# Layer 1 of a spectral/MLP block on one core: the d transform split by frequency modulo four, with new orders of work

## The chip, the cores and the metric

The kernel runs on one core of a Trainium2 chip. The metric is device time in microseconds (us): the median of six runs is 348.16 us (347.78 to 348.58). The core has TensorE (PE in the profile; PEld is its weight load), VectorE (DVE), ScalarE (ACT), GpSimd (POOL) and SyncE (SP, which only starts transfers).

## The reference

`x` is 2048 x 512 in bf16. Two kinds of layer alternate, twice each.

```python
x = A_x
x = x + _A_ref(_layernorm(x), A_w_r, A_w_i)
x = x + _B_ref(_layernorm(x), B_w1, B_w2, B_w3, B_w4)
x = x + _A_ref(_layernorm(x), A_w_r, A_w_i)
x = x + _B_ref(_layernorm(x), B_w1, B_w2, B_w3, B_w4)

def _A_ref(x, w_r, w_i):          # 2048 x 512 -> filter -> 2048 x 512
    X = rfft2(x.astype(float32))  # 2048 x 257 frequencies
    return irfft2(X * (w_r + 1j * w_i)).astype(bfloat16)

def _B_ref(x, w1, w2, w3, w4):
    h = gelu(layernorm(x) @ w1)                  # 512 -> 512
    hs = (four quarters of h, shifted by -1, +1, -2, +2 along 2048) @ w2
    x1 = x + hs
    return x1 + gelu(layernorm(x1) @ w3) @ w4    # 512 -> 1792 -> 512
```

"Layer 1" below is the first A and the first B; "layer 2" the second pair.

## The kernel before

The 2048 positions are written as 128 `p` times 16 `q`; a "row" q is a 128 x 512 tile, held in `K.x` for the whole kernel. The Fourier transforms are matrix products with tables. Layer A runs through six stages.

1. p transform (letter O in the orders). In layer 1 `first_front` takes the mean and variance of each row (s, i, f), the inverse deviation of a group of rows (S on ScalarE, J on VectorE), scales the table `T` by it (Q, on VectorE or ScalarE) and multiplies. `over_p` (L386 to L396) forms, for each of two blocks t of 128 columns, x[t]·T and x[t+2]·(T, -T) in one accumulation: the four matmuls of a row have 256 columns each and leave the sum and the difference of the two halves of the row. G (`take_V`) copies the result from PSUM into `V`, whose first index (four blocks of 128 d) is 2t + h, where h = 0 holds sums and h = 1 differences.
2. d transform (letter d, `over_d`, L504 to L512). Even frequencies need only the sums, odd ones only the differences, so for each of 16 frequency blocks b there are four matmuls of 256 columns (two h, two t) with the table `FA`. t copies the result to `TV`.
3. q transform (q, L535, table `TL` and its turned copy; x copies the result to `X`).
4. Filter (p, `weigh`, L554, VectorE only, weights `W`).
5. Inverse q (b, L565, table `TR`; m copies to `hT`), inverse d (D, L583, table `G`; Y copies) and inverse p (P, L595).
6. a adds the result to the row (L603); s, r, e, i, n form the next layer norm, T sends pairs of rows through a DMA transpose.

Blocks are handled in units: b = 0, 1, 14 and 15 alone ("singles"), the rest in pairs ("doubles"). Layer B then runs w1 (v, L635), w2 (u, L651), w3 (w, L686) and w4 (W, L706). Near its end the front of layer 2 is mixed in (the same letters O and G).

What runs when is written out by hand: `ORDER_0` (layer 1's front), `ORDER_A` (the rest of layer 1) and `ORDER_B` (layer 2) list operations as a letter, a number and, where there is a choice, the engine (V = VectorE, A = ScalarE). Each engine executes its own operations in that order and never overtakes. The number behind a point is the first PSUM bank. X is a number of filling matmuls on zeros (`fill`, 256 columns each); `WAKE` of them open the kernel and `FILL` puts some behind blocks of the first front.

Transfers: SyncE loads `x` (8 transfers), then the weights `W` (16), then, behind a gate that waits for the last part of W, `G`, `Tinv` and w1 to w4, then a dummy transpose. GpSimd's queue holds, in this order: the sums of rows 1 and 5, the loads of `FA`, `TL` (two halves) and half of `TR`, a doubling of the first quarter of `W` (a copy to the odd partitions), a gate that waits for the last scaled table, the turning of the first half of `TL` (L233, L234), the doubling of W's second quarter, the turning of the second half of `TL`, the last two doublings, and the rest of `TR`.

Rows 1 and 5 have their mean and square summed on ScalarE (`ON_ACT`, L349 and L285, finished by three small GpSimd operations); the other rows use VectorE's statistics instruction (L273, L301).

Of the kernel before, what the change touches and what calls it, by code (L numbers as in the profile page):

```python
# [28 lines left out]
def dft_tables():  # L29
# [27 lines left out]
    FA = np.stack([cos, -sin], axis=1).reshape(2, P, 2, P, 2)[..., ::-1].transpose(1, 0, 4, 2, 3)  # L57
    w = np.full(256, 2.0)
# [33 lines left out]
    out = {"T": np.stack([T, -T], axis=1), "FA": FA, "TL": TL, "TR": TR, "G": G, "G2": G2,  # L92
# [62 lines left out]
def load_all(K, A_x, A_w_r, A_w_i, B_w1, B_w2, B_w3, B_w4):  # L155
# [24 lines left out]
    def load_rest(after):  # L180
        q = nc.gpsimd
        load_TL = lambda k: q.dma_start(K.TL[:, 0, 8 * k:8 * k + 8], dram["TL"][:, 8 * k:8 * k + 8])
        load_TR = lambda k: q.dma_start(K.TR[:, 0:2 + k, 16 * k:16 * k + 16], dram["TR"][:, 0:2 + k, 16 * k:16 * k + 16])
        double = lambda k: q.dma_start(K.W[1::2, :, 8 * k:8 * k + 8], K.W[0::2, :, 8 * k:8 * k + 8])
        table("FA", q)
        load_TL(0)
        load_TL(1)
        load_TR(0)
        double(0)
        gate = K.const.tile([1, 2], BF16, name="gate")  # L190
        q.tensor_copy(gate[:], after[0:1, 0, 0:2])
        turn_TL(K, slice(0, 8))
        double(1)
        turn_TL(K, slice(8, 16))
        double(2)
        double(3)
        load_TR(1)

    K.load_rest = load_rest
    K.load_G2 = lambda: nc.sync.dma_start(K.G[:], dram["G2"])  # L200

    def load_mlp():
# [4 lines left out]
        for k, w, n, c in (("w1", B_w1, 4, D), ("w2", B_w2, 4, D), ("w3", B_w3, 4, FH), ("w4", B_w4, 14, D)):  # L207
            t = K.const.tile([P, n, c], BF16, name=k)
            nc.sync.dma_start(t[:], w.rearrange("(t p) n -> p t n", p=P))
            setattr(K, k, t)  # L210

# [185 lines left out]

def over_p_plain(K, qs):
# [34 lines left out]
def first_front(K):  # L433
# [30 lines left out]
    def front(k):  # L464
        ps[k] = over_p(K, FIRST[k], k == len(FIRST) - 1)
        if k in FILL:
            fill(K, FILL[k])

# [3 lines left out]
    def means(g):  # L472
        for i, q in enumerate(GROUPS[g]):
            if q in ON_ACT:
                L[g].from_means(i)

# [9 lines left out]
    spare = K.grp.tile([P, 4, 4, P], BF16, name="xT", bufs=4)  # L486
    K.nc.sync.dma_start_transpose(spare[:, 0, 0:1], K.zeros[:])


def layer(K, last):  # L490
# [13 lines left out]
    def over_d(u):  # L504
        bs = UNITS[u]
        ps["d", u] = o = banks(K, len(bs))
        for i, b in enumerate(bs):
            oi = o[:, i].rearrange("p (e h f) -> p h e f", e=2, h=2)
# [6 lines left out]
    def take_d(u, eng):  # L515
# [5 lines left out]
        else:  # L521
            copy(K, tv[u][:].rearrange("p n (e f h) -> p (n e) f h", e=2, h=2),
                 src.rearrange("p n (e h f) -> p (n e) f h", e=2, h=2), eng)
# [287 lines left out]
s0 s2 i0 s3 s1 i2 i3 f0 s4 S0 J0 i4 s5 Q1V Q0V Q3V Q2V s7 s6 i7 i6 s9 s11 O0 G0A f1 i9 S1 J1 s8 O1 G1A Q6A s10 Q7A i11  # L811
O3 i8 i10 Q5A s13 s12 Q4A O2 S2 J2 i13 Q10V G3A i12 Q9V s15 Q11A O5 S3 Q8A s14 i15 G2A O4 i14 S4 J3 Q12V G5A J4 Q15A
Q13V O6 Q14V G6A G4V O7 G7V O8 G8V G8A
"""
ORDER_A = """
X4.1 N0 d0.3 t0A d2.5 d1.7 t1A d4.0 t4A q0.2 x0A t2V q1.4 x1V p1 d10.6 d6.4 p0 t6V q2.1 t10A q4.6 x2A p2 x4A d12.3
b1.0 q6.1 p4 q10.6 t12A m1V b3.3 m3V x6A d8.4 d14.2 d15.0 x10A b5.6 t8A q8.4 p6 t14V t15A q12.0 b2.7 p10 m2V q14.2 m5A
x8A x12A q15.4 b0.6 m0A b10.7 m10A b4.1 m4A p8 b6.0 p12 m6V x14A p14 b11.7 x15A b9.1 p15 b13.6 m11A m9V m13A b7.3
b12.5 m12A b8.2 m8A b14.7 m14A m7V b15.5 m15A m15V D1.1 Y1V D0.5 D3.3 P2.7 a2 P3.2 a3 Y0A P0.1 a0 Y3A P7.4 P1.7 a1 s2
P6.2 s3 D2.0 s0 s1 a7 s7 a6 s6 D5.3 D4.6 r0 e0 Y2V P4.5 Y5A Y4A i0 n0V n1V P5.0 a4 s4 a5 s5 P11.2 D7.4 r1 P10.6 T0 Y7A  # L820
P8.3 e1 n3V n2V c1 T1 a11 a8 i1 D6.0 Y6A n5V P9.4 s11 P14.7 n4V n6V a9 n7V T2 P15.5 P12.3 a10 s8 a15 s9 a14 s10 P13.0
L0 v0.1 h0 a12 a13 v1.5 h1 T3 r2 c2 v3.4 n11V s12 c0 n10V T5 n8V n9V h3 s15 v2.3 h2 u0.5 L8 u3.0 u2.7 f0 L2 s14 f3
u1.5 f1 s13 r3 n12V n14V n15V f2 T4 v5.2 n13V h5 v4.1 u4.5 f4 E1 h4 u7.6 u6.1 f7 E3 u5.4 T7 k1 k0 f6 f5 k3 k2 E5 R0 c3
T6 v7.5 h7 u15.7 E0 v6.0 h6 E6 E4 u8.4 k7 o0V k5 o1V f15 E2 k6 o2V u10.3 o3V f10 k10 u12.7 u11.0 f8 u14.1 f14 U0 U1
u9.2 f9 k9 k8 w2.4 g2 f12 L9 E9 k4 R1 f11 k11 R2 w5.6 E11 g5 w4.2 g4 w1.0 u13.4 E8 o8V g1 o9V w3.5 g3 f13 E10 o10V
w0.1 g0 E7 o4A o7V w6.3 g6 W2.2 z0 o5V o6V A2 W3.7 A3 W1.6 A1 B1 W0.2 U3 U4 U2 E14 A0 w8.6 L13 B3 j3 g8 k14 o11V w12.1
g12 U5 w13.6 g13 w7.3 g7 w9.6 g9 k15 w10.3 g10 w18.0 w15.3 E12 g18 g15 w14.6 g14 w16.0 L11 w11.3 g11 g16 B2 W6.2 E13
W4.0 A6 w20.5 k13 L5 A4 B4 L12 W7.0 g20 w17.4 k12 R3 g17 o13A W5.1 A5 w19.5 g19 W9.2 o12V U6 j1 A7 B7 L15 j7 E15 j2 L7
o15V B6 W8.1 j6 B0 B5 j5 L3 W10.7 j0 S0 A10 B10 o14A U7 A9 j10 w25.4 g25 B9 Q2 j4 j9 A8 B8 L1 S1 Q1 Q4 w24.6 g24 W11.0
w21.2 g21 Q6 w22.6 j8 A11 L4 Q0 Q7 B11 j11 g22 L10 O0.3 w26.1 L14 g26 S2 Q11 G0A Q3 w23.6 w27.0 Q9 G0V g23 O1.2 G1A  # L830
Q10 G1V g27 W12.5 A12 O3.0 B12 W15.6 j12 Q5 G3A G3V A15 O2.2 G2A B15 Q8 j15 G2V S15 J15 Q15 W13.5 A13 B13 S12 W24.4
A24 j13 S13 J12 Q12 B24 J13 W14.5 Q13 A14 B14 O4.0 G4A O15.2 j14 S14 O5.6 G15V G15A O6.4 J14 Q14 O14.2 G4V G5A X3.7
G14V L6 G6A X4.1 G14A
"""
ORDER_B = """
d1.1 d4.3 t1V d15.7 t15V d8.0 t8V t4A q1.2 x1A p1 q4.6 x4A p4 d12.4 q15.2 t12A d10.6 x15A p15 t10A q8.0 q12.4 x12A
b1.2 m1A d14.6 d2.3 t14A x8V p12 t2A d0.0 t0A b5.2 m5A p8 q10.5 x10V p10 q2.3 x2A d6.0 t6A b9.2 p2 b4.3 m9A q0.4 x0A
p0 q14.6 m4A x14A q6.0 x6A b13.2 b12.4 m12A b10.3 b0.7 m0A p14 b3.5 m3A b2.0 m13A m10V p6 b14.3 b11.4 m2V b8.6 m11A
m8A b7.5 b6.4 m14V m6A m7V b15.1 m15A m15V D3.4 Y3A D2.6 D1.1 Y2A P6.3 a6 Y1A s6 D0.4 P4.6 Y0A P5.7 P7.3 a4 s4 P3.1 a5
s5 a7 s7 a3 r1 P2.0 a2 P0.7 a0 s3 P1.3 a1 s2 e1 i1 n4V D5.4 D7.1 D4.6 Y5A P11.3 P10.0 n5V D6.4 n7V n6V s0 s1 r0 Y7A e0  # L840
Y4V P8.6 P9.2 T2 P14.1 a10 i0 c1 n2V n3V Y6A s10 a11 n1V P15.0 n0A s11 a9 a8 s9 s8 c0 r2 T3 P13.7 a13 P12.5 a12 T1
v3.3 h3 v2.6 h2 s12 n10V T0 v1.2 n8V n9V T4 v0.4 s13 n11V h1 u3.7 a14 T5 h0 a15 u1.6 f1 u0.0 s15 u2.4 f2 s14 r3 n14V
n15V T7 n12V v5.2 h5 v4.1 h4 u4.5 n13V E1 k1 u6.4 f3 E3 f0 E0 u7.3 k2 u5.7 k3 k0 c2 f7 T6 v6.2 h6 v7.1 h7 E2 f5 u13.6
R0 u12.0 E7 o2V u14.7 o3V o1V f6 o0V c3 f12 U0 f13 u15.2 f15 k15 f4 f14 E14 E15 E6 k13 k12 u9.0 f9 u10.1 k14 U1 w2.4
g2 w4.6 k4 f10 R3 k10 E13 w0.1 g0 w6.3 E12 o12A g4 w1.1 g1 g6 w3.5 g3 w5.1 g5 u11.5 E4 k5 f11 W2.3 E11 o13V o14A k7 U6
o15A k11 W1.4 A1 k6 R1 u8.2 A2 f8 k9 k8 R2 o6V U7 w25.6 g25 w22.3 o4V E10 o10A g22 E5 o5V w21.0 W3.2 A3 g21 w24.5 g24
# [35 lines left out]
```

## Time and profile before

One execution was profiled. It took 347.91 us, of which the traced span is 346.1 us; the granted TensorE clock is 1.00.

| stretch (us) | what runs |
|---|---|
| 0 to 18.4 | loads, layer 1's front: statistics, p transform |
| 18.4 to 38.1 | layer 1's d, q, filter and inverse q |
| 38.1 to 52.8 | layer 1's inverse d and p, layer norm, transposes |
| 52.8 to 179 | layer 1's B, at its end layer 2's statistics and part of its p transform |
| 179 to 183.2 | the rest of layer 2's p transform |
| 183.2 to 202.8 | layer 2's d, q, filter and inverse q |
| 202.8 to 218.2 | layer 2's inverse d and p |
| 218.2 to 342.7 | layer 2's B |
| 342.7 to 346.1 | last addition and store |

In a timeline row the columns are start, length, engine, line, operation, output and inputs, count, and in brackets the idle time before it with what ended it. The length of a matmul row contains the drain of the last one, so the pitch is read from start to start.

### The profile page before, as it was taken

The numbers are of one execution on the slowest core, as the hardware profiler recorded it, in microseconds if no ns is written. First come the engines' busy times: TensorE is split into PE (matmuls) and PEld (weight loads), VectorE is DVE, ScalarE is ACT, GpSimd is POOL, SyncE is SP. The second block draws the span as 40 slices with busy tenths as digits, with TensorE's granted clock in tenths as the row PEclk, the third lists the DMA queues.
The fourth block names the chain that finished last, engine by engine and source line by source line (L and its number), as shares of the span: only waits on it lengthen the run. The fifth ranks groups of instructions, "written<-read, shape, count | busy, mean of one in ns | idle before, by whom it ended". The sixth has DMA issues, their size and how long they took to land.

```text
span 346.1 us, 5563 instructions
## 1 busy us (share of the span) xinstructions
PE 336.7 (97%) x2116; PEld 189.6 (55%) x2134; DVE 187.7 (54%) x452; ACT 192.0 (55%) x342; POOL 64.5 (19%) x158
## 2 busy tenths in 40 slices
PE   8899999999999999999999999999999999999996
PEld 6778884444444444444577888444444444444453
DVE  5979798785435012877698959666614202002012
ACT  5979799666505633124357989954784521350320
POOL 2470047442200001022000003544304000000000
PEclk9999999999999999999999999999999999999999
DMA  7998965430221000310000002542103114100101
GB/s 256 282 336 273 370 112 110 78 63 2 53 40 30 0 2 0 57 36 1 0 2 2 0 2 54 95 86 50 24 2 61 30 45 105 19 29 17 45 23 53
DMA packets 45337, 24.64 MB, mean 71 GB/s; under 512 B 34944, under 2 KB 42240, under 8 KB 45312
## 3 DMA queue, kind: packets, MB, share of 16 engines
q1 hardware_dynamic: 43904, 20.00, 23.4%
q0 software_dynamic: 1168, 4.20, 3.4%
q8 instruction: 16, 0.26, 0.3%
q10 hardware_dynamic: 240, 0.10, 0.2%
q14 instruction: 9, 0.07, 0.1%
HBM read 11.67 MB, written 2.10 MB: 40 GB/s over the span
## 4 chain that ended last, share of the span: by engine, by line
PE 78%; DMA 9%; DVE 7%; ACT 2%; SPq 1%; issue 1%; ACTq 0%; DVEq 0%; POOLq 0%
PE ps L686 28%; PE ps L706 27%; PE ps L635 8%; PE ps L651 8%; DMA W<-in_A_w_i_dram 4%; DVE x_state L603 3%; PE ps L511 2%; DMA xT<-xn 2%; PE ps L583 2%; DVE PB L554 1%; DMA W<-in_A_w_r_dram 1%; PE ps L535 1%; DMA W<-W 1%; ACT hT L152 1%; DVE xn L369 1%
## 5 line engine op out<-in xcount | busy, mean ns | idle before, releaser
L693 ACT ACTIVATE gT<-ps 128x1024 bf16<-128x1024 f32 x56 | 56.3, 1021 | 93.9 <-PE ps L686 93.7
L686 PE MATMUL ps<-xT,w 128*128 128x512 bf16 x448 | 99.3, 379 | 0.1
L706 PE MATMUL ps<-w,gT 128*128 128x512 bf16 (+1 forms) x464 | 97.8, 366 | 0.6
L712 DVE TENSOR_TENSOR x_state<-ps,x_state 128x512 bf16<-128x512 f32 (+1 forms) x34 | 22.1, 657 | 108.5 <-PE ps L706 106.8
L706 PEld LDWEIGHTS <-gT 128*128 128x128 bf16 x476 | 46.4, 98 | 49.9
L686 PEld LDWEIGHTS <-w 128*128 128x128 bf16 x448 | 43.8, 98 | 52.6 <-DMA xT<-xn 0.2
L659 DVE SCALAR_TENSOR_TENSOR xn<-xn,ln_c,ps 128x512 bf16<-128x512 bf16 x32 | 23.2, 743 | 21.5 <-PE ps L651 13.1
L635 PE MATMUL ps<-xT,w 128*128 128x512 bf16 x128 | 28.8, 379 | 1.0 <-DMA xT<-xn 1.0
L651 PE MATMUL ps<-w,hT 128*128 128x512 bf16 x122 | 28.6, 379 | 0.3
L285 ACT ACTIVATE junk<-xn 128x512 bf16<-128x512 bf16 x32 | 19.7, 620 | 10.0 <-DVE xn L659 10.0
L642 ACT ACTIVATE hT<-ps 128x512 bf16<-128x512 f32 x32 | 18.1, 600 | 11.8 <-PE ps L635 11.8
L603 DVE SCALAR_TENSOR_TENSOR x_state<-ps,x_state 128x512 bf16<-128x512 f32 x32 | 20.5, 686 | 5.1 <-PE ps L595 5.1
L273 DVE BATCH_NORM_STATS2 ln_st<-x_state 128x6 f32<-128x512 bf16 (+1 forms) x31 | 20.1, 665 | 3.4 <-DMA x_state<-in_A_x_dram 3.0
L635 PEld LDWEIGHTS <-w 128*128 128x128 bf16 x128 | 12.4, 98 | 16.2 <-issue 1.8
L651 PEld LDWEIGHTS <-hT 128*128 128x128 bf16 x128 | 12.5, 98 | 15.1
L291 POOL TENSOR_SCALAR ln_mv<-ln_s 128x4 f32<-128x4 f32 x16 | 4.9, 304 | 84.5 <-DVE x_state L603 72.4
L554 DVE TENSOR_TENSOR PB<-X,W 128x2048 bf16<-128x2048 bf16 (+1 forms) x20 | 19.6, 1008 | 0.7 <-ACT X L152 0.5
L285 ACT ACTIVATE xn<-x_state 128x512 bf16<-128x512 bf16 x32 | 19.8, 622 | 0.2 <-DVE x_state L603 0.2
L293 POOL TENSOR_TENSOR ln_mv<-ln_s,ln_t 128x4 f32<-128x4 f32 x16 | 3.7, 233 | 75.7 <-ACT junk L285 70.3
L583 PE MATMUL ps<-G,hT 128*128 128x256 bf16 x128 | 15.4, 272 | 0.9 <-DVE hT L150 0.8
L565 PE MATMUL ps<-TR,PB 128*128 128x128 bf16 x256 | 16.1, 219 | 0.1
L565 PEld LDWEIGHTS <-PB 128*128 128x128 bf16 x256 | 14.8, 98 | 1.5 <-issue 1.2
(87 smaller groups left out, 387.6 us busy)
## 6 DMA issues: line engine op xcount, KB each, us to landing
w<-in_B_w_dram SPq DMA_DIRECT2D x2, 1792.0 KB, 12.5
W<-W POOLq DMA_DIRECT2D x4, 514.0 KB, 4.6
x_state<-in_A_x_dram SPq DMA_DIRECT2D x8, 256.0 KB, 5.1
out_dram<-x_state SPq DMA_DIRECT2D x15, 128.0 KB, 1.8
w<-in_B_w_dram SPq DMA_DIRECT2D x2, 512.0 KB, 5.5
W<-in_A_w_r_dram SPq DMA_DIRECT2D x7, 128.5 KB, 7.1
W<-in_A_w_i_dram SPq DMA_DIRECT2D x7, 128.5 KB, 6.6
TR<-tab_TR POOLq DMA_DIRECT2D x1, 768.0 KB, 6.1
```

The lines of the kernel that those rows point to most:

```text
L285: K.nc.scalar.activation(out, src, ACT.Square, bias=0.0, scale=D ** -0.5, accum_out=self.s[:, i, 1:2])
L554: nc.vector.tensor_tensor(t, X.pop(u)[:, 0:2 * n].unsqueeze(1).to_broadcast([P, 2, 2 * n, 256]), K.W[:, :, 2 * u:2 * u + 2 * n, 1:257], op ...
L565: nc.tensor.matmul(oh, lhsT=pab[u][:, k, 2 * (b - u) + h, F * P:(F + 1) * P], rhs=K.TR[:, k:k + 2, 2 * b + h], start=(k == 0), stop=(k == 1))
L583: nc.tensor.matmul(o[:, i, e * 256:(e + 1) * 256], lhsT=M[:, F, e, 2 * m + i, :], rhs=K.G[:, F, e, :], start=(F == 0 and e == 0), stop=(F ...
L603: nc.vector.scalar_tensor_tensor(K.x[:, q, :], ps.pop(("P", q)), 1.0, K.x[:, q, :], op0=ALU.mult, op1=ALU.add, accum_out=ln[g].s[:, i, 0:1])
L635: nc.tensor.matmul(o[:, i], lhsT=K.w1[:, t, j * P:(j + 1) * P], rhs=xT[g][:, :, t, :], start=(t == 0), stop=(t == 3))
L651: nc.tensor.matmul(o, lhsT=K.hT[:, j, st:st + P], rhs=K.w2[:, j, :], start=(j == 0), stop=(j == 3))
L659: nc.vector.scalar_tensor_tensor(xn[:, q, :], xn[:, q, :], ln[q // 4].c[:, q % 4:q % 4 + 1], ps.pop(("u", n)), op0=ALU.mult, op1=ALU.add, ...
L686: nc.tensor.matmul(o[:, i], lhsT=K.w3[:, c, t * P:(t + 1) * P], rhs=xT3[g][:, :, c, :], start=(c == 0), stop=(c == 3))
L693: nc.scalar.activation(gT[g][:, 2 * j:2 * j + 2, :], ps.pop(("w", k)), ACT.Gelu_apprx_tanh, bias=0.0, scale=1.0)
L706: nc.tensor.matmul(o, lhsT=gT[g][:, t, i * P:(i + 1) * P], rhs=K.w4[:, t, d], start=(t == 0), stop=(t == 13))
L712: nc.vector.tensor_tensor(x, ps.pop(("W", n)), x, op=ALU.add)
```

## The change

Layer 1 only, arithmetic: the p transform adds the four quarters of a row in all the combinations that the d transform needs. `V` then holds x0 - x2, x0 + x1 + x2 + x3, x0 - x1 + x2 - x3 and x1 - x3. Frequencies 0 modulo 4 need one block of 128 d, frequencies 2 modulo 4 one block, odd frequencies two blocks. A row of the p transform has eight matmuls (four of 256 and four of 128 columns); a block b of the d transform has two of 128 and two of 256 columns.

```diff
+def over_p_quarters(K, qs, split=False):
+    ps = banks(K, 2 if split else len(qs))
+    for i, q in enumerate(qs):
+        T = K.Tq.pop(q)
+        plus, both, swap = T[:, 0], T[:], T[:, ::-1]
+        twice = lambda k: T[:, k:k + 1].to_broadcast([P, 2, P])
+        for h in range(2):
+            o = (ps[:, h, 0:256] if split else ps[:, i, h * 256:(h + 1) * 256]).rearrange("d (k p) -> d k p", k=2)
+            terms = ((0, o, twice(0)), (1, o[:, 1], plus), (3, o[:, 1], plus), (2, o, swap)) if h == 0 else \
+                    ((1, o, swap), (0, o[:, 0], plus), (2, o[:, 0], plus), (3, o, twice(1)))
+            for n, (c, dst, rhs) in enumerate(terms):
+                K.nc.tensor.matmul(dst, lhsT=K.x[:, q, c * P:(c + 1) * P], rhs=rhs, start=(n == 0), stop=(n == 3))
+    return ps
...
-        ps[k] = over_p(K, FIRST[k], k == len(FIRST) - 1)
+        ps[k] = over_p_quarters(K, FIRST[k], k == len(FIRST) - 1)
...
+            if not last:
+                oi = o[:, i].rearrange("p (e r f) -> p e r f", e=2, r=4)
+                part = lambda k: V[:, k, 2 * b:2 * b + 2].rearrange("d b q c -> d (b q c)")
+                nc.tensor.matmul(oi[:, :, 3], lhsT=part(1), rhs=K.FL[:, 0:P].rearrange("p (e f) -> p e f", e=2),
+                                 start=True, stop=True)
+                nc.tensor.matmul(oi[:, :, 1], lhsT=part(2), rhs=K.FL[:, P:2 * P].rearrange("p (e f) -> p e f", e=2),
+                                 start=True, stop=True)
+                for k in range(2):
+                    rhs = K.FL[:, (k + 1) * 256:(k + 2) * 256].rearrange("p (e r f) -> p e r f", e=2, r=2)
+                    nc.tensor.matmul(oi[:, :, 0:3:2], lhsT=part(3 * k), rhs=rhs, start=(k == 0), stop=(k == 1))
+                continue
```

The copies t of layer 1 read PSUM with four interleaved classes instead of two; their size stays. The new table `FL` (128 x 768, 192 KB) is loaded into a spare transpose buffer where `FA` (256 KB) was loaded, right behind the sums of row 5 on GpSimd's queue; `FA`, which only layer 2 uses now, comes on SyncE's queue behind w4. The turned second half of `TL` is loaded as a table of its own (`TL2`, 256 KB) instead of being formed by two GpSimd operations. Row 9's sums go to ScalarE, with three small operations on GpSimd ahead of the first doubling.

```diff
+    def load_tables():
+        spare = K.grp.tile([P, 4, 4, P], BF16, name="xT", bufs=4)
+        K.FL = spare[:, 0:2].rearrange("p a b c -> p (a b c)")[:, 0:768]
+        q.dma_start(K.FL, dram["FL"])
         load_TL(0)
         load_TL(1)
         load_TR(0)
...
         turn_TL(K, slice(0, 8))
         double(1)
-        turn_TL(K, slice(8, 16))
+        q.dma_start(K.TL[:, 1, 8:16], dram["TL2"])
         double(2)
         double(3)
...
-WAKE = 35
-FILL = {0: 3, 1: 3, 2: 2, 3: 2, 4: 2}
+WAKE = 30
+FILL = {}
-ON_ACT = [1, 5]
+ON_ACT = [1, 5, 9]
+TABLES = 1
```

All three orders are written anew. `ORDER_0` whole, and `ORDER_A` as far as the first D (the first lines of each):

```diff
 ORDER_0 = """
-s0 s2 i0 s3 s1 i2 i3 f0 s4 S0 J0 i4 s5 Q1V Q0V Q3V Q2V s7 s6 i7 i6 s9 s11 O0 G0A f1 i9 S1 J1 s8 O1 G1A Q6A s10 Q7A i11
-O3 i8 i10 Q5A s13 s12 Q4A O2 S2 J2 i13 Q10V G3A i12 Q9V s15 Q11A O5 S3 Q8A s14 i15 G2A O4 i14 S4 J3 Q12V G5A J4 Q15A
-Q13V O6 Q14V G6A G4V O7 G7V O8 G8V G8A
+s0 s3 s2 i3 s1 f0 i0 i2 S0 s5 f1 J0 Q0V Q1V Q2A Q3A s4 i4 s6 s7 i6 i7 O0 G0A S1 s10 J1 s12 Q6A s9 Q7V s13 i12 i13 Q4V
+s8 S3 O1 G1A Q5V O3 J3 O2 i10 G3A Q12V s11 i8 i11 Q13V O6 f2 S2 J2 G2A Q10V Q11V Q8V O5 G6A Q9A O4 s15 s14 i15 i14 S4
+J4 Q14V O7 G5A Q15V G4A O8 G8A G7V G8V
 """
 ORDER_A = """
-X4.1 N0 d0.3 t0A d2.5 d1.7 t1A d4.0 t4A q0.2 x0A t2V q1.4 x1V p1 d10.6 d6.4 p0 t6V q2.1 t10A q4.6 x2A p2 x4A d12.3
-b1.0 q6.1 p4 q10.6 t12A m1V b3.3 m3V x6A d8.4 d14.2 d15.0 x10A b5.6 t8A q8.4 p6 t14V t15A q12.0 b2.7 p10 m2V q14.2 m5A
-x8A x12A q15.4 b0.6 m0A b10.7 m10A b4.1 m4A p8 b6.0 p12 m6V x14A p14 b11.7 x15A b9.1 p15 b13.6 m11A m9V m13A b7.3
-b12.5 m12A b8.2 m8A b14.7 m14A m7V b15.5 m15A m15V D1.1 Y1V D0.5 D3.3 P2.7 a2
...
+d0.3 t0V d1.6 d2.0 t1A q0.2 x0V p0 t2A q1.4 x1A p1 d4.6 N0 t4A d10.1 t10A q2.4 x2V p2 q4.6 d6.0 x4A t6A d12.3 t12A
+d14.5 q10.6 q6.0 d8.2 p4 x10A b4.4 x6V b3.7 d15.6 t8A q8.2 m4A t15A p10 p6 q12.0 b1.4 m3A b0.6 b2.7 x8A x12A b6.2 m2A
+t14V b5.3 m1V p8 q15.0 m0A q14.4 b10.7 x15A b9.6 p12 m6A m10V p15 b8.0 m5A x14A b7.2 m7A b11.3 p14 b12.7 m8V b13.5 m9V
+b14.1 m11A m12A b15.2 m13A m14A X4.0 m15A m15V D1.5 Y1A D0.0 Y0A D3.3 Y3A P2.5 a2
...
```

`ORDER_B` has the same operations as before, in another order and with some copies t, x and m given to the other engine: ScalarE has 9 double copies, 16 copies of 512 columns and one half in layer 2's stretch from the first d to the first D, where it had 9, 17 and one half.

## Prediction

> **What bounds the kernel now.** I read the page's first part, then busy time by stage, then the timelines of TensorE, VectorE and ScalarE up to 40 us, last the chain of waits. Busy time by stage (stretch, its length, busy time and instructions of TensorE, weight load, VectorE, ScalarE, GpSimd; clock, DMA share, GB/s):
>
> ```profile
> 7.50:16.90 9.40, 8.14 (x70) 6.72 (x70) 9.29 (x33) 8.71 (x18) 4.28 (x10) 1.00 0.93 291
> 16.90:29.00 12.10, 11.82 (x130) 9.45 (x129) 10.27 (x14) 9.85 (x14) 6.94 (x8) 1.00 0.89 316
> 29.00:38.00 9.00, 8.64 (x141) 7.62 (x138) 8.95 (x12) 8.84 (x16) 0.00 (x0) 1.00 0.95 317
> 52.90:80.00 27.10, 27.00 (x124) 12.22 (x127) 21.01 (x60) 18.60 (x45) 13.84 (x33) 1.00 0.40 76
> ```
>
> From 52.9 us on TensorE alone is full, and the change leaves its matmuls there alone. Up to 38 us three engines are nearly full together: what one gives up counts only if the others follow. The matmuls in the timeline of TensorE:
>
> ```profile
> 7.56 0.27 PE L392 MATMUL ps<-Tq,x_state 128*128 128x256 bf16 x1 [0.47 <-DVE Tq L379]
> 11.30 0.27 PE L392 MATMUL ps<-Tq,x_state 128*128 128x256 bf16 x1 [1.18 <-ACT Tq L381]
> 17.50 0.27 PE L394 MATMUL ps<-Tq,x_state 128*128 128x256 bf16 x1
> 18.42 2.78 PE L511 MATMUL ps<-FA,V 128*128 128x256 bf16 x24
> 38.09 2.78 PE L583 MATMUL ps<-G,hT 128*128 128x256 bf16 x24 [0.46 <-DVE hT L150]
> ```
>
> So the front runs to 18.42, and d to the first D is 19.67 us. Pitches of matmuls come from pieces of the chain of waits, which follow without a gap (layer 2):
>
> ```profile
> 192.33 0.45 PE ps L565 x8
> 192.78 0.98 PE ps L535 x16
> 206.04 0.87 PE ps L583 x8
> ```
>
> 128 columns 0.056 us, 256 columns 0.109 us, the half-height q matmuls 0.061 us, weight loads hidden. TensorE's work in the 19.67 us is 64 x 0.109 (d) + 64 x 0.061 (q) + 128 x 0.056 (b) = 18.0 us, so 1.7 us of waits.
>
> ScalarE and VectorE (timelines):
>
> ```profile
> 7.03 0.87 DVE L379 TENSOR_SCALAR Tq<-T,ln_r 128x256 bf16<-128x256 bf16 x4
> 9.23 1.25 DVE L273 BATCH_NORM_STATS2 ln_st<-x_state 128x6 f32<-128x512 bf16 x2
> 19.12 0.60 ACT L152 ACTIVATE TV<-ps 128x512 bf16<-128x512 f32 x1 [0.91 <-PE ps L511]
> 24.19 1.94 ACT L152 ACTIVATE X<-ps 128x1024 bf16<-128x1024 f32 x2 [0.35 <-PE ps L535]
> 35.12 3.06 ACT L152 ACTIVATE hT<-ps 128x512 bf16<-128x512 f32 x6
> ```
>
> Start to start: statistics 0.59, scaled table 0.20 on VectorE and 0.42 on ScalarE, a double copy on ScalarE 0.91, a single one or an m 0.48. ScalarE's copies between 19.12 and 37.95 (letters t, x, m with an A): 10 doubles x 0.91 + 15 singles x 0.48 + a half of 0.35 = 16.65 us in 18.83 us, 2.2 us of waits.
>
> **The front.** Removed: twelve fills (1.3 us). Added: four 128-column matmuls per row; a row is now 4 x 0.109 + 4 x 0.056 = 0.66 us, where it was 0.44: 16 rows 10.6 us instead of 7.0. TensorE has idled or filled for about 3 us in its 10.2 us here, which would just hide the 3.6 us if the rows came evenly. They do not. I lay out `ORDER_0` by the pitches:
>
> - Row 0's table is the first to be scaled and J0 no longer stands behind s4: row 0 starts at about 7.28 (now 7.56), rows 0 and 1 end at 8.60, rows 2 and 3 (tables scaled on ScalarE behind row 5's sums, 8.0 to 8.85) at 9.94.
> - ScalarE copies G0A until 9.75, S1 to 10.05, J1 on VectorE 10.2, Q6A 10.75: row 6 starts at 10.8 (now 11.30).
> - From there twelve rows stand end to end: 12 x 0.66 = 7.9 us, and 0.2 for row 5, whose scaling stands behind s8: 18.9. Now the last row ends at 17.6. The statistics and scalings of VectorE end at 17.4 by the same pitches (14 changes to 13 statistics, 9 to 12 scalings) and are no longer last; row 9's two sums on ScalarE (1.3 us, by rows 1 and 5) lie in 10.75 to 12.05, where only G1A stands behind them, with 0.4 us left before row 12 needs its bank.
> - Last copies as now (17.72 to 18.42): d starts at 19.6, **1.2 us later**. Bounds: +0.6 if row 6 starts half a microsecond sooner, +1.8 if each of the three bank waits costs 0.2.
>
> No row has a matmul that adds 128 columns into half of an open accumulation. b's 128-column row (0.056) is the nearest; the 256-column pitch is the upper bound, +0.053 x 64 = 3.4 us. I take the nearest.
>
> The Trainium skill speaks against this step: "TensorE: Matmul & The Clock Gate", section "Back-to-back issue gap", gives about 81 ns per matmul of N=128 in a stream of weight load and matmul pairs. The trace's b stream is such pairs, at 0.056. By the page the front would be an estimated 1.6 us longer still; the measurement decides.
>
> **d to the first D, layer 1.** d loses 16 x (4 x 0.109 - 2 x 0.109 - 2 x 0.056) = 1.7 us, so TensorE's work is 16.3 us. But ScalarE now has 10 doubles, 16 singles and the half, 17.1 us, starting at 0.91 (d0, d1, 0.25 to the copy). Floor: 0.91 + 17.1 + 0.14 (last m to D) = 18.2. Laid out bank by bank ScalarE waits about 0.7 more: I take **18.9, 0.8 us less** than 19.67. Bounds: 18.2 and, with all of today's 2.2 us of waits, 20.4. Interleaving four classes on read is the same number of elements; between zero (the two-class copy has the same 0.91 as layer 2's plain one) and 0.23 each, the gap between VectorE's and ScalarE's double copy, for eight doubles: 1.8. I take zero.
>
> **Transfers and GpSimd.** Two turning operations go (1.66 + 0.78 us), a transfer comes (0.6 us of issue). GpSimd's queue: the three operations for row 9 (0.6 us) delay the first doubling to about 13; its user p0 runs at 22. What follows is the gate (16.3), the first turn (to 18.9, needed by q0 at 21), the second doubling, then `TL2` at 19.5; like `TL` (5.8 us to landing) it lands at 25.3. Its first user, q10, is at 19.6 + 6.6 = 26.2: hidden by 0.9 us, and a stall of 1.2 us if it takes the 7.9 us that half of `TR` took on this queue. The third doubling goes out 1.7 us sooner, or waits for W as now. `FL` is 64 KB smaller than `FA`. On SyncE, `FA` costs an issue of 0.5 us and, with `TL2`, 0.45 MB, at 350 GB/s 1.3 us of queue ahead of the dummy transpose; weights drain now at 45, the first transpose starts at 47.3, so it is covered by 2 us; uncovered, it delays w1 (52.8) one for one.
>
> **The rest.** From the first D to w1 the order of VectorE, which leads to the transposes, is the same but for Y1, which goes to ScalarE off the path: 0, bounds 0.4 either way. B is TensorE end to end with the same matmuls: 0. Layer 2's d to D has no new work; ScalarE's first copy comes at 2.0 instead of 1.57, with 16.2 instead of 16.7 us of copies: -0.1, bounds -0.5 to +0.5. Tail: the last store still follows the last addition (A20 before y20): 0.
>
> **Sum** against the profiled 347.91: +1.2 - 0.8 - 0.1 = +0.3, 348.2. The profiled run lies 0.25 under the median of 348.16; on the median 348.4. This kernel's runs tell about 0.2% (0.7 us) from no change, and +0.3 is inside.
>
> **Rivals.**
> 1. Faster. The columns taken from d pay in full and the front hides the added ones: front +0.6, stage at its floor (-1.5), layer 2's rewritten order -0.4: -1.3, 346.9. For: the 3 us of idling and fills in the front; TensorE's share in 18 to 38. Against: twelve rows end to end.
> 2. Slower. ScalarE is the bound of the stage. It has 0.5 us more copies and keeps today's waits: the stage is 20.1, +0.5, and the front's +1.2 is not returned: +1.6, 349.8. For: 16.65 of 18.83 us busy already. It decides once ScalarE waits over 1.3 us between first copy and D (stage 19.5, total +0.9).
> 3. Slower. `TL2` is late for q10: on top of the forecast up to 1.2 us, 349.6, once it needs more than 6.7 us to land.
> 4. The clock: fills are gone and TensorE idles about 0.7 us before 7.3 and 0.9 before 10.8. If the clock falls, some 3 us at half speed, +1.5: 349.9. Against: 1.18 us idle before 11.30 now, clock 1.00.
>
> **Numbers.** Forecast 0.38 (its own range 347.6 to 349.0), rival 1 0.32, rival 2 0.21, rivals 3 and 4 0.09 together. Range 346.5 to 350.2: the sums of rivals 1 and 4 and 0.3 beyond; costlier copies or matmuls lie outside. Faster 0.32, same 0.38, slower 0.30.
>
> **What would show it.** Right: d starts at 19.2 to 20.0 with rows end to end from about 10.8; the first D 18.6 to 19.2 later; q10 waits for no transfer; first w1 at 53.2 and the same distance from there to the end as now. Wrong: d before 19.0, a pitch of L424's matmuls over 0.66 per row, the stage under 18.2 or over 19.7, a clock below 1.00 before 20 us, or more than 0.5 us gained or lost behind w1.

## The result, and the profile after

The changed kernel took 348.87 us (median of 21 runs, 348.22 to 350.48); the kernel before, in 42 runs beside it, 348.28 us (347.71 to 350.13). The ratio is 1.0019 with a 95% interval of 1.001 to 1.0027: slower by some 0.6 us, at the 0.2% that this kernel's measurement can tell from no change. The forecast was 348.4, with a range of 346.5 to 350.2.

The execution that was profiled took 349.64 us, 0.77 above its own median, so its rows can't be set against those of before without care. Two things in it are chance, and shown below: its input came late, and its transposes were held. First the busy time by stage of the kernel after (stretch, its length, busy time and instructions of TensorE, weight load, VectorE, ScalarE, GpSimd; clock, DMA share, GB/s):

```profile
7.70:19.90 12.20, 11.13 (x129) 9.78 (x128) 10.65 (x37) 11.46 (x23) 5.89 (x13) 1.00 0.98 308
19.90:38.60 18.70, 18.39 (x260) 15.13 (x261) 17.14 (x22) 17.38 (x27) 4.22 (x7) 1.00 0.86 280
38.60:54.17 15.57, 14.49 (x129) 12.44 (x130) 11.86 (x36) 14.38 (x33) 5.29 (x17) 1.00 0.96 251
184.53:204.58 20.05, 19.15 (x256) 16.37 (x257) 18.83 (x23) 17.03 (x26) 0.00 (x0) 1.00 0.01 2
204.58:219.12 14.54, 14.46 (x128) 12.40 (x129) 11.64 (x32) 12.53 (x29) 2.25 (x10) 1.00 0.20 38
219.12:344.19 125.07, 124.22 (x582) 57.63 (x590) 37.24 (x93) 57.15 (x99) 20.29 (x52) 1.00 0.22 44
344.19:347.90 3.71, 0.00 (x0) 0.00 (x0) 0.42 (x1) 0.00 (x0) 0.00 (x0) 1.00 0.34 108
```

And the stages of layer 2 in the kernel before, from its own profile:

```profile
183.21:202.82 19.61, 19.17 (x256) 16.01 (x257) 18.02 (x22) 17.26 (x27) 0.00 (x0) 1.00 0.01 2
202.82:218.18 15.36, 14.51 (x128) 12.44 (x129) 11.20 (x35) 14.30 (x32) 4.57 (x15) 1.00 0.25 47
218.18:342.73 124.55, 124.04 (x581) 57.63 (x590) 36.35 (x93) 54.76 (x95) 18.74 (x48) 1.00 0.20 44
342.73:346.10 3.37, 0.00 (x0) 0.00 (x0) 0.42 (x1) 0.00 (x0) 0.00 (x0) 1.00 0.18 58
```

The reader is to see that layer 1's stage from d to the first D (second row) shrank to 18.70, that the next one (third row) grew to 15.57 from 14.75, that layer 2's d to D takes 20.05 where it took 19.61, and that more time passes behind the last addition. (The last rows reach to the span as it is printed, to 0.1 us; to the last instruction it is 3.67 us where it was 3.37.) The granted clock is 1.00 everywhere.

TensorE's timeline of the kernel after:

```profile
7.73 2.80 PE L424 MATMUL ps<-Tq,x_state 128*128 128x256 bf16 x32 [1.57 <-DVE Tq L393]
11.33 8.36 PE L424 MATMUL ps<-Tq,x_state 128*128 128x256 bf16 x96 [0.80 <-ACT Tq L395]
19.90 0.22 PE L542 MATMUL ps<-xT,V 128*128 128x128 bf16 x1 [0.21 <-ACT V L159]
38.60 2.79 PE L625 MATMUL ps<-G,hT 128*128 128x256 bf16 x24
54.17 7.07 PE L677 MATMUL ps<-xT,w 128*128 128x512 bf16 x32 [0.89 <-DMA xT<-xn]
```

Twelve rows of eight matmuls (x96) stand end to end from 11.33 without a wait of any length, just as it was laid out: 8.36 us with the drain of the last one, so 8.2 without (0.27 of a matmul less its pitch of 0.109), 0.683 per row on the mean. Nine of the twelve take 0.66.

When the input lands differs from execution to execution. The first statistics wait for it. VectorE's first row, kernel before and then kernel after:

```profile
3.94 1.50 DVE L273 BATCH_NORM_STATS2 ln_st<-x_state 128x6 f32<-128x512 bf16 x2 [2.98 <-DMA x_state<-in_A_x_dram]
```

```profile
4.57 1.96 DVE L287 BATCH_NORM_STATS2 ln_st<-x_state 128x6 f32<-128x512 bf16 x3 [3.62 <-DMA x_state<-in_A_x_dram]
```

So 0.63 us of the later d are the input's. In all profiled executions of both kernels and of the variants below, the first statistics start between 3.94 and 4.57. The table therefore counts from them (all times in us; each column is one profiled execution; E4 and E7 are variants told of below):

| from, to | before | before, again | after | E4 | E7 |
|---|---|---|---|---|---|
| first statistics to d, layer 1 | 14.48 | 14.34 | 15.33 | 15.32 | 15.33 |
| d to first D, layer 1 | 19.67 | 19.67 | 18.70 | 18.81 | 18.70 |
| first D to first w1 | 14.75 | 14.81 | 15.57 | 14.52 | 14.76 |
| first statistics to first w1 | 48.90 | 48.82 | 49.60 | 48.65 | 48.79 |
| w1 to d of layer 2 | 130.37 | 130.37 | 130.36 | 130.52 | 130.37 |
| d of layer 2 to last addition | 159.52 | 159.46 | 159.66 | 159.20 | 159.34 |
| last addition to last instruction | 3.37 | 3.40 | 3.67 | 3.04 | 3.03 |
| of that, to the end of the last store's packets | 1.64 | 1.64 | 1.84 | 1.63 | 1.64 |

Layer 1's front is 0.85 to 0.99 us longer and its d stage 0.86 to 0.97 shorter, so up to the first D the two cancel. What the kernel after lost lies behind that.

### The profile page after: what moved, and what is told of

It reads as the page before. It is cut to its first block, busy times and chain, and to the rows that moved or that the text cites. A ratio compares the mean times of both kernels' runs of the same rounds, so it can differ in the third digit from the quotient of the medians.

```text
span 347.9 us, 5683 instructions
## 1 busy us (share of the span) xinstructions
PE 336.9 (97%) x2164; PEld 190.4 (55%) x2181; DVE 185.9 (53%) x445; ACT 198.2 (57%) x351; POOL 61.9 (18%) x160
## 4 chain that ended last, share of the span: by engine, by line
PE 77%; ACT 9%; DVE 7%; DMA 4%; issue 2%; DVEq 0%; ACTq 0%
PE ps L728 28%; PE ps L748 28%; PE ps L693 8%; PE ps L677 7%; ACT xn L299 3%; DMA xT<-xn 2%; DVE ln_st L287 2%; PE ps L607 2%; DVE PB L596 1%; ACT V L159 1%; PE ps L625 1%; ACT hT L159 1%; PE ps L577 1%; ACT Y L159 1%; DVE X L157 1%
## 5 line engine op out<-in xcount | busy, mean ns | idle before, releaser
L287 DVE BATCH_NORM_STATS2 ln_st<-x_state 128x6 f32<-128x512 bf16 (+1 forms) x30 | 19.6, 664 | 3.9 <-DMA x_state<-in_A_x_dram 3.6
L305 POOL TENSOR_SCALAR ln_mv<-ln_s 128x4 f32<-128x4 f32 x16 | 5.9, 368 | 81.9 <-DVE x_state L645 68.3
L607 PE MATMUL ps<-TR,PB 128*128 128x128 bf16 x256 | 16.3, 219 | 0.3 <-DVE X L157 0.3
L159 ACT ACTIVATE TV<-ps 128x1024 bf16<-128x1024 f32 (+1 forms) x16 | 14.2, 915 | 4.0 <-PE ps L553 2.3
```

Source lines behind the costliest of these rows:

```text
L159: K.nc.scalar.activation(dst, src, ACT.Copy, bias=0.0, scale=1.0)
L287: self.K.nc.vector.bn_stats(self.st[i][:, int(k)], src)
L607: nc.tensor.matmul(oh, lhsT=pab[u][:, k, 2 * (b - u) + h, F * P:(F + 1) * P], rhs=K.TR[:, k:k + 2, 2 * b + h], start=(k == 0), stop=(k == 1))
```

## The experiments

The first group asks how the loss divides among the parts: the place of `FA`'s load, the turned table, the new order of layer 2, and the new arithmetic. Each kernel computes the whole reference. "Before" in brackets is the kernel before, measured beside it.

**E1: `FA` loaded later.** Only the place of the load of `FA` is changed: from behind w4 to ahead of `G2`, after the dummy transpose and the transposes.

```diff
-    K.load_G2 = lambda: nc.sync.dma_start(K.G[:], dram["G2"])
+    def load_G2():
+        table("FA", nc.sync)
+        nc.sync.dma_start(K.G[:], dram["G2"])
...
-        table("FA", nc.sync)
```

> The changed kernel with FA moved on SyncE's queue from behind w4 to ahead of layer 2's G, far behind the transposes of layer 1. Theory A (the changed kernel loses about 0.8 us between layer 1's first D and w1 because the first transposes stand behind 0.45 MB more and a later gate): first transpose issued without the 2.9 us hold, D to w1 back from 15.6 towards 14.8, median 348.1 to 348.5, smaller spread. Rival B (the loss is the front's, the late w1 belongs to that one execution): D to w1 unchanged on the whole, median 348.7 to 349.0.

Measured: 348.57 us (348.13 to 349.47, 12 runs; before 348.32), ratio 1.0007, interval 0.9997 to 1.0017. That is 0.3 under the kernel after, and the two intervals overlap, so by time alone nothing is settled. The profiles show what the load can do. SyncE's queue at the first transposes of layer 1, kernel before, then the kernel after (columns: start, length of the issue, queue, line, what, count):

```profile
47.27 1.26 SPq L623 DMA_TRANSPOSE xT<-xn  x1
```

```profile
47.80 2.93 SPq L665 DMA_TRANSPOSE xT<-xn  x1
```

And the queues around them in the kernel after (stretches of 1 us):

```profile
46.00:47.00 1.00, 0.81 (x9) 0.58 (x6) 0.92 (x2) 1.00 (x4) 0.00 (x0) 1.00 1.28 365
...
49.00:50.00 1.00, 1.00 (x12) 0.90 (x10) 0.86 (x3) 1.00 (x5) 0.64 (x3) 1.00 2.59 130
```

In the kernel before the DMA share (the time that packets took; where they overlap it can pass 1, as in the last row) is already 0.12 in 45 to 46 and 0.00 in 46 to 48; here the weights flow at 365 GB/s until 47 and at 105 in 47 to 48, and the first transpose is issued at 47.80. Its issue is held 2.93 us instead of 1.26, the second stands behind it, and w1 waits 0.89 (the timeline above). With `FA` loaded late the flow falls to 95 GB/s in 46 to 47, and w1 waits for nothing. But the hold is not there each time: of four profiled executions with `FA` behind w4 (after, E2, E4, E6) two have it (after, 2.93 us; E6, 3.23 us, where w1 waits 1.81).

The landing times tell more than the flow. On the queue the dummy transpose stands ahead of the first real one. In the kernel before it lands at 46.66, 0.6 us before the first real one is issued; with `FA` behind w4 it lands after that issue, by 3.65 us (after) and 3.95 (E6) where the hold was, and by 2.84 (E4) and 2.68 (E2) where the issue took 1.75 and 1.67. In E1 it lands 1.11 us behind the issue, which takes 1.73. So the late tables make the hold possible, and it was longest where the dummy landed latest; the landing isn't all of it, since the second profile of the kernel before has 1.23 with an issue of 1.26.

**E2: the second half of `TL` turned by GpSimd again.**

```diff
-        q.dma_start(K.TL[:, 1, 8:16], dram["TL2"])
+        turn_TL(K, slice(8, 16))
```

> The changed kernel with the second half of the q table turned by GpSimd again instead of loaded. Theory A (the 256 KB of TL2 stand between the doublings of W and make the gate of the MLP weights 2.4 us late): last doubling lands near 27.3 instead of 29.7, weights and transposes 2 us sooner, median 348.2 to 348.6; q10 waits for no turning, which ends near 24.5. Rival B: same as the changed kernel, 348.7 to 349.0. Rival C (the load was worth it): q10 waits, 349.3 or more.

Measured: 349.56 us (349.33 to 349.85, 8 runs), ratio 1.0031, interval 1.002 to 1.0042: 0.7 slower than the kernel after. The transfer earns its place, and not by what it does to GpSimd's queue. VectorE and GpSimd in E2:

```profile
22.32 2.27 DVE L596 TENSOR_TENSOR PB<-X,W 128x1024 bf16<-128x1024 bf16 x2
```

```profile
21.14 1.67 POOL L247 TENSOR_SCALAR TL<-TL 128x512 bf16<-128x512 bf16 x1
22.70 0.79 POOL L248 COPY TL<-TL 128x512 bf16<-128x512 bf16 x1
```

and the same weighing in the kernel after, where GpSimd turns nothing at that time:

```profile
22.80 1.30 DVE L596 TENSOR_TENSOR PB<-X,W 128x1024 bf16<-128x1024 bf16 x2
```

The same two weighings take 2.27 us instead of 1.30 while GpSimd works on tables, 0.97 more. All of it is in the first one, which takes 1.67 instead of 0.70; the second starts at 23.92, when GpSimd's copy has ended (23.49), and takes 0.68. TensorE pays it a little later (d waits 0.58 for VectorE's copy at 26.12), and E2's stage from d to D is 19.68 us instead of 18.70: 0.98 more. In the kernel before the turning ended at 21.84 and the weighings began at 22.52, at 1.30 the pair, so the old order did not pay. The new front holds the turning back until the last table is scaled, 1.6 us later, and without the transfer it meets the weighings. So the number of Rival C came, but not by its reason: q10 is not what waits.

**E4: the kernel after with the old order of layer 2.** `ORDER_B` is put back whole; its first line, new and old:

```diff
-d15.7 t15V d4.1 t4V d1.3 t1A d8.6 q1.4 x1V t8A p1 q4.2 x4A q15.0 x15V p4 d12.4 t12A d10.6 q8.2 p15 q12.4 t10A x12A
+d1.1 d4.3 t1V d15.7 t15V d8.0 t8V t4A q1.2 x1A p1 q4.6 x4A p4 d12.4 q15.2 t12A d10.6 x15A p15 t10A q8.0 q12.4 x12A
```

> The changed kernel with layer 2's old order, ORDER_B of the kernel before. Theory A (layer 2's new order costs 0.3 to 0.5 us: d to D 20.05 instead of 19.61, D to w1 0.8 shorter but a wait inside w1, tail 0.3 longer): median 348.3 to 348.6. Rival B (the two orders are worth the same, as forecast to 0.1): 348.8 to 349.0. Rival C (the new order is the better one): 349.2 or more.

Measured: 347.53 us (347.1 to 348.92, 12 runs; before 348.32), ratio 0.998, interval 0.9969 to 0.9992. It is 1.3 us faster than the kernel after, more than was expected, and faster than the kernel before. So layer 1's part of the change is a gain, and the new `ORDER_B` takes more than it back (about 0.3 of the 1.3 lie in the end of the program, which is told of last and isn't shown to be the order's). Where, the chain of waits shows (start, length, engine and what it made). Kernel after, layer 2's q and filter:

```profile
187.69 0.70 DVE X L157
188.40 0.02 issue
188.42 0.71 DVE PB L596
...
193.01 2.38 DVE PB L596 x2
...
195.51 1.24 DVE X L157
196.75 0.04 issue
196.79 1.05 PE ps L607 x16
```

E4, the same place (its d starts at 183.53, that of the kernel after at 184.53):

```profile
187.08 0.98 PE ps L553 x8
188.06 0.33 PE ps L577 x4
188.38 0.98 PE ps L553 x8
189.36 0.98 PE ps L577 x16
...
194.07 0.98 PE ps L553 x8
195.05 0.89 PE ps L607 x16
```

With the old order TensorE itself is the chain here. With the new one VectorE is: it copies x and weighs in turn with hardly a gap from 187.69 to 196.75, and TensorE waits twice for its copies of x, 0.13 us at 188.44 and 0.31 at 196.79, the latter in its timeline:

```profile
196.79 1.05 PE L607 MATMUL ps<-TR,PB 128*128 128x128 bf16 x16 [0.31 <-DVE X L157]
```

E4 and the kernel before have neither wait, and the two together are the whole difference between 20.05 and 19.61. The new order gives VectorE the copies x1 and x15, which were ScalarE's, near the start of the stage, and x0 later, all of them ahead of weighings that only VectorE can do; ScalarE gets t1 and one m for them. Every profile with the new order, six in all, has 20.05 from d to D, every one with the old, seven in all, 19.61. Which of the moves makes the two waits was not tried one by one.

**E5b: the kernel before with the new `ORDER_B` alone.** The mirror image of E4.

> The kernel before with only ORDER_B, layer 2's order, taken from the changed kernel. Theory A (ORDER_B alone loses about 1 us: VectorE's chain in d to D 0.45, a transpose waited for inside w1 0.35, the last store 0.3): 349.1 to 349.6. Rival B (the old order only suits the changed layer 1 better): 348.1 to 348.6.

Measured: 349.33 us (348.23 to 349.93, 9 runs; before 348.25), ratio 1.0027, interval 1.0016 to 1.0039. The new order costs the old kernel 1.1 us, as E4 gained 1.3 by dropping it. Its profiled execution has the same 20.05 us from d to D and the same waits of 0.13 and 0.31 for VectorE's copies. It also has a wait that no other profile shows: w1 of layer 2 stands 0.98 us at 236.93 for a transpose that was issued at 232.14 and landed at 236.88. Its runs spread over 1.7 us, so the 1.1 may hold some of that.

**E6: the stores at the end.** In the new `ORDER_B` the stores of rows 14 and 10 stand between that of row 11 and the last one; here they go ahead of row 11's addition.

```diff
-... W10.6 A10 y9
-W11.5 A11 W20.6 y11 y14 y10 A20 y20
+... W10.6 A10 y9 y14 y10
+W11.5 A11 W20.6 y11 A20 y20
```

> The changed kernel with the stores of rows 14 and 10 (first halves) issued ahead of row 11's instead of between it and the last one. Theory A (two stores of 0.4 us issue stand in front of the last store after row 11's addition): last store issued right behind the last addition, 348.5 to 348.7. Rival B (the tail is not set by the issue): 348.8 to 349.0.

Measured: 348.28 us (347.89 to 349.92, 12 runs; before 348.25), ratio 1.0007, interval 0.9997 to 1.0017; 0.6 under the kernel after, but the intervals overlap. The profile is clearer than the time, though it is of the execution that took 349.92, with the transposes held. From the last addition to the last instruction it has 3.46 us, where the kernel after has 3.67, and the last store's packets end 1.63 us behind the start of the addition instead of 1.84. SyncE behind the last addition, kernel after and then E6 (last additions at 344.19 and 344.68):

```profile
343.38 1.80 SPq L758 DMA_DIRECT2D out_dram<-x_state  x4
```

```profile
345.13 0.33 SPq L758 DMA_DIRECT2D out_dram<-x_state  x1
```

Four stores queue up in the one, until 345.18, 0.57 after the addition has ended; in the other the last store goes out by itself as soon as its row is there and takes 0.33.

**E5: the new orders with the old arithmetic.** `over_p` and `FA` for layer 1 in place of the quarters and `FL`; all orders and the rest as after, `FA` loaded once, early.

```diff
-        ps[k] = over_p_quarters(K, FIRST[k], k == len(FIRST) - 1)
+        ps[k] = over_p(K, FIRST[k], k == len(FIRST) - 1)
...
-            if not last:
+            if False:
```

> The changed kernel with the old arithmetic: p transform by halves, d by parity, FA loaded where FL was and no longer behind w4; new orders, TL2, row 9's sums stay, fills stay out. Theory A (the quarters cost the front 1 us and give the stage 0.8 to 1.0, about nothing net; without FA behind w4 the transposes are sooner): d starts at 18.4 to 18.8, stage 19.5 to 19.9, median 348.1 to 348.6. Rival B (the quarters gain in the stage more than they cost): 349.3 or more. Rival C (they cost): 347.7 or less.

Measured: 350.62 us (349.0 to 350.72, 6 runs; before 348.32), ratio 1.0053, interval 1.0035 to 1.0071. First statistics to d: 15.15 us, only 0.18 less than with the quarters, although TensorE has half as many matmuls there, with two thirds of the columns, which now wait for scaled tables (the last such wait is 0.44, for VectorE, at 18.05). The new front is therefore bound nearly as late by statistics and scalings as by its matmuls. The d stage is 19.50 us, 0.8 more than with the quarters: what they save lies in d. The rest of the loss is not the arithmetic's by anything shown here: the new `ORDER_B` is in it, and in its profile w1 of layer 1 waits 1.15 us at 58.34 for rows whose transpose landed at 58.20, a wait that no other profile has in that size.

**E8: the quarters alone.** The kernel before with `over_p_quarters`, `FL` and the new d, without fills, `FA` ahead of `G2`; the old orders, row 9 on VectorE and GpSimd's turning stay.

```diff
-        ps[k] = over_p(K, FIRST[k], k == len(FIRST) - 1)
+        ps[k] = over_p_quarters(K, FIRST[k], k == len(FIRST) - 1)
...
-FILL = {0: 3, 1: 3, 2: 2, 3: 2, 4: 2}
+FILL = {}
```

> The kernel before with the quarters alone: p transform by quarters, d by frequency modulo four, FL for FA (FA ahead of G2), no fills between rows; all old orders, the second half of TL turned, row 9 on VectorE. Theory A (twelve rows of 0.66 us from 11.3 end at 19.3, d starts at 19.8 to 20.0 instead of 18.4; stage 0.6 to 1.0 shorter): 348.6 to 349.2. Rival B (the quarters pay by themselves): 347.7 or less. Rival C (ScalarE holds the stage at 19.7): 349.5 or more.

Measured: 349.34 us (349.04 to 349.44, 6 runs; before 348.25), ratio 1.0032, interval 1.002 to 1.0044. First statistics to d 16.16 us, d to D 19.13. So the arithmetic shows no gain by itself, and neither do the new orders of layer 1: E5 less the cost of `ORDER_B` (1.1 by E5b) and its wait of 1.15 is about the kernel before. By E7 and E9, told of next, the quarters need a front that starts rows early; that the d stage needs copies dealt out anew is read off 19.13 against 18.70 and was not tried by itself.

**E7: the best of these together.** The kernel after with the old `ORDER_B` and `FA` ahead of `G2` (E1 and E4).

> The changed kernel with layer 2's old order and FA moved ahead of G2. Theory A (the two corrections add: 347.5 less 0.3): 347.0 to 347.4. Rival B (FA's place is worth nothing): 347.4 to 347.8.

Measured: 347.56 us (347.3 to 348.6, 11 runs; before 348.25), ratio 0.9982, interval 0.9972 to 0.9992. It beats both kernels and equals E4, with a narrower spread; `FA`'s place adds nothing to the median here.

**E9: row 9 back on VectorE.** E7 with `ON_ACT = [1, 5]`, and `i9` (VectorE) in `ORDER_0` where `f2` stood.

```diff
-ON_ACT = [1, 5, 9]
+ON_ACT = [1, 5]
```

> The changed kernel with layer 2's old order, FA ahead of G2, and row 9's statistics back on VectorE in the same place (behind row 6's scaling, its variance ahead of S2). Against the same kernel with row 9 on ScalarE, 347.56. Theory A (rows stand end to end from row 6 on, so 0.6 us more on VectorE ahead of row 7's and row 5's scaling moves the rows and d by 0.4 to 0.8): d starts at 19.8 to 20.2, 347.9 to 348.4. Rival B (row 9 is hidden on either engine): d at 19.4, 347.4 to 347.7.

Measured: 349.25 us (348.9 to 350.17, 5 runs; before 348.13), ratio 1.0034, interval 1.0021 to 1.0048: 1.7 slower than E7 and more than either expectation. First statistics to d 16.10 us, 0.77 more than E7's 15.33, and the matmuls no longer stand end to end:

```profile
11.19 1.64 PE L427 MATMUL ps<-Tq,x_state 128*128 128x256 bf16 x16 [0.80 <-ACT Tq L398]
13.00 2.99 PE L427 MATMUL ps<-Tq,x_state 128*128 128x256 bf16 x32 [0.17 <-DVE Tq L396]
16.22 4.12 PE L427 MATMUL ps<-Tq,x_state 128*128 128x256 bf16 x48 [0.23 <-DVE Tq L396]
```

Moving one row's statistics off VectorE buys 0.8 us of front, more than its 0.59 us of work: two waits for scaled tables and a later end come with it. Up to w1 it is 0.99 (49.78 from the first statistics, against 48.79), with a wait for the transposes. Another 0.45 lies behind the last addition (3.48 us against 3.03), where E7 lacks a pause that is told of next; nothing ties it to row 9's sums.

**The kernel before and E7 once more,** to see the same places twice.

> The kernel before once more, for a second profile of it. Theory A (up to layer 2's first d the two layers 1 cost the same within 0.2 us, so the 0.7 us by which the changed kernel with the old ORDER_B wins lie behind that: the transposes of layer 2 and the tail): first w1 at 52.8 to 53.0, layer 2's d at 183.2 to 183.4, last addition to end 3.3 to 3.4. Rival B (the before's typical execution is later in layer 1 than the one profiled): first w1 at 53.2 or later.

> The changed kernel with the old ORDER_B and FA ahead of G2 once more, for a second profile. Theory A: first w1 at 52.7 to 53.0, last addition to end 3.0 to 3.1, as in its first profile. Rival B (that tail was chance): 3.3 to 3.4.

Measured, one run each: 348.22 and 347.73 us. From first statistics to w1 48.82 and 48.63; counted from zero w1 is at 53.21 and 53.13, later than Theory A had it, since the input landed late in both (first statistics at 4.39 and 4.50). From the last addition to the last instruction 3.40 and 3.04. The last pair was met before: 3.37 in the first profile of the kernel before, 3.03 in E7 and 3.04 in E4, although these kernels have the same last stores. The DMA view of the end tells them apart (busy tenths in 40 slices from 342.5 to 349, so past the end of either span, and the queues of that window). Kernel before:

```profile
DMA  0299100004800000000000020000000000000000
q1 hardware_dynamic: 288, 0.20, 9.5%
q14 instruction: 1, 0.01, 0.5%
```

E7:

```profile
DMA  2992000038100000000000000000000000000000
q1 hardware_dynamic: 288, 0.20, 9.4%
```

Behind the last store (the pair 48, 38) the kernel before has one more small transfer, the "2", on the queue that brings instructions; E7 has none. The transfer can't be what the program waits for: it starts at 346.38, and the last instruction has ended at 346.11. What lengthens the span is a pause of 0.32 us between two of GpSimd's last instructions, 345.35 to 345.67, where E7 has no gap above 0.07. All ten profiles with the transfer have one such pause, of 0.32 to 0.37, and the transfer starts 1.02 to 1.08 us behind its beginning; the three without it (E4, E7, E7 again) have no pause. The ten end 3.34 to 3.72 us after the last addition's start, the three after 3.03 to 3.04.

The stores are apart from that. With the four stores of the new `ORDER_B` the last packet ends 1.83 to 1.84 us after the start of the last addition (five profiles), in all the others, E6 included, after 1.63 to 1.64. So the stores cost 0.2, and the pause goes with 0.3 to 0.4. What brings the pause and the transfer was not tried.

## Why the prediction was right or wrong

- **Front, +1.2, d at 19.6.** Right, and a little too high. Counted from the first statistics the front grew by 0.85 to 0.99; d starts at 19.41 to 19.68 in E1, E4 and E7, and at 19.90 after with the late input. Row 6 was put at 10.8 and starts at 10.83 in E7; twelve rows took 8.2 us where 7.9 and 0.2 were laid out. That is 0.683 per row, above the 0.66 that was named as a sign of being wrong; nine rows kept 0.66, and the 0.3 more lie in three rows between 12.6 and 15.6. The sum was high by 0.3 in the last copies: 0.38 from the last matmul's pitch to d in E7, where 0.7 was taken. The price per matmul, 0.056 us for 128 columns into half of an open accumulation, held. The estimated 1.6 us that the Trainium skill's 81 ns ("TensorE: Matmul & The Clock Gate", section "Back-to-back issue gap") would have added did not come.
- **VectorE no longer last.** Right by little. In E5, with half the matmuls, d comes only 0.18 sooner: scalings and row copies end almost as late.
- **d to D, 18.9.** Right: 18.70 to 18.81. The way there was another. ScalarE does not wait between its first copy and its last. These are four rows of its timeline after; of all its rows in the stage only the first has an idle time in brackets:

```profile
21.14 1.68 ACT L159 ACTIVATE TV<-ps 128x512 bf16<-128x512 f32 x2 [1.37 <-PE ps L548]
23.20 1.95 ACT L159 ACTIVATE TV<-ps 128x1024 bf16<-128x1024 f32 x2
30.95 2.08 ACT L159 ACTIVATE X<-ps 128x1024 bf16<-128x1024 f32 x2
35.95 2.87 ACT L159 ACTIVATE hT<-ps 128x512 bf16<-128x512 f32 x6
```

  Its first copy starts 1.24 after d (0.91 was taken), from there it has no gap above 0.06, and the last copy but one ends at 38.55, 0.05 before D: 1.24 + 17.41 + 0.05 = 18.70. So ScalarE was the bound, as named, but the 0.7 of waits laid out bank by bank were really 0.33 of a later start and copies that took longer than by their pitches (17.20 for 16.8 up to the start of the last one). Four interleaved classes cost at most that. One reading was wrong: 37.95 is not the end of ScalarE's copies in the kernel before (the last runs from 37.78 to 38.19) but that of VectorE's last hT, for which D waits there. The chain of waits before that D is VectorE's weighings and copies; in the kernel after it is ScalarE's copies, in E4 first the one and then the other. The two engines end nearly together.
- **TL2.** Right: its issue came at 21.57 and not at 19.5, since the gate ahead of it waits for the last scaled table (18.41, not 16.3), but it took 4.2 us to land, not 5.8: 25.8, and q10 started at 26.61 without a wait. What was missed is its worth. Turning on GpSimd was counted on GpSimd's queue alone; E2 shows that VectorE's weighing takes 0.97 us longer when they meet.
- **`FA` behind w4, "covered by 2 us".** The cover was mis-sized. The 2 us were read from the flow, which is all but over at 45; w4 lands at 46.35 and the dummy transpose at 46.66, so the cover was 0.6 us to begin with. And the gate that lets the weights go moved by 2.4 us, from 27.25 to 29.66. It goes with the second doubling of `W`, which is issued at 20.90 instead of 18.80, behind the longer front; in E2, without the load of `TL2`, the gate is passed at 29.70 as well. With that and 1.3 us of queue for two tables, the flow ends at 47 to 48, on top of the transpose, and `FA` lands at 51.17. In two of the profiled executions w1 is 0.9 and 1.8 us late; with its late input the kernel after has w1 at 54.17 and not at 53.2. This may be part of why the kernel after spreads to 350.48.
- **Layer 2, -0.1, "no new work", and the tail, 0.** This is the step that failed. The forecast weighed ScalarE's copies, 16.2 us instead of 16.7, and not VectorE, which got what ScalarE gave up, in front of weighings that nobody else can do. By the table's row the stretch from layer 2's d to the last addition is 0.14 to 0.20 longer than before and 0.3 to 0.5 longer than with the old order in the same kernel (1.3 in E5b, 0.98 of it the one wait for a transpose). Inside it d to D is 0.44 longer, the two waits for VectorE. The tail was judged by the last store alone ("still follows the last addition"), not by what is queued on SyncE ahead of it: 0.2. In medians the order costs 1.1 (E5b) to 1.3 us (E4), the latter with the pause of the end, 0.3, that E4 lacks.
- **The rivals.** Faster fails in each of its terms: the front grew by 0.85 to 0.99 and not 0.6, the stage lost 0.86 to 0.97 and not 1.5, and layer 2 didn't gain. Yet the kernel without the new `ORDER_B` is faster by 0.7 us, about half of which goes with the pause that it lacks. Slower because ScalarE keeps its waits: refuted, it has none behind its first copy. `TL2` late: refuted. The clock: 1.00 in every stage.

The total of 348.87 lies inside the range and 0.5 above the forecast (348.16 and 0.3 make 348.46, so 0.4 above its own terms). This is no proof of the sum: layer 1, for which +0.4 was forecast, is worth about -0.2 up to w1 where the transposes aren't held, and layer 2 with the tail, for which -0.1 was forecast, costs +0.4 to +0.5 (0.43 from w1 to the end, just under the 0.5 that was named as a sign of being wrong), and the hold sometimes adds 0.9 to 1.8. Two errors of opposite sign partly cancelled; that the total came so close is luck.

What stays open: of the 0.7 us by which E4 and E7 beat the kernel before, 0.34 to 0.37 go with the pause at the end that they lack, and 0.1 to 0.3 with layer 1; the rest is within what single profiled executions can resolve. Open too are when the hold of the first transpose falls on an execution, and what brings the pause.

## What to carry to other kernels

When an order of work is rewritten "with the same operations", add up each engine's share by its own pitches, above all that of the engine that alone can do some of the work. Here one copy moved off ScalarE, which had the time to spare, onto VectorE, which then led the stage. A cover measured before a change is no cover after it if its start is moved by the same change: follow the gate, not the clock time, and measure it by landing, not by flow. And put apart the parts of a change that share no data: the one that was meant to matter gained 0.5 us (the kernel after against E5b) to 0.7 (E4 against the kernel before), and its companion lost 1.1 to 1.3.

## What the runs showed of the hardware

- VectorE's product of two bf16 tiles was held beside GpSimd's work: 1.67 us instead of 0.70 while GpSimd turned a table, and 0.68 for the next one when GpSimd had ended (E2). Copies out of PSUM beside the same kind of work were not: 0.42 us for the copy of 256 columns at 19.31 in E2, while GpSimd turned the first half.
- The issue of a transpose on SyncE's queue is no fixed price: 1.26 or 1.27 us in the five profiles in which the transpose ahead of it had landed before its issue or up to 1.2 us behind, and 1.67 to 3.23 in the eight in which that landed 1.1 to 4.0 us behind. The longest two, 2.93 and 3.23, are those with the latest landing (3.65 and 3.95).
- The end of the program carries a price that no line of it shows: in ten of thirteen profiles GpSimd pauses for 0.32 to 0.37 us between its last instructions, and a transfer on the queue that brings instructions starts some 1.05 us after the pause begins.
- Input lands at times that differ by 0.6 us from execution to execution (first statistics at 3.94 to 4.57), and the whole kernel moves with it. In differences of half a microsecond, count from the first statistics and not from zero.
